# Where an early first layer puts its sums: three PSUM tiles in turn, or four banks of one tile

## The chip, the cores and the metric

The kernel runs on one core of a Trainium2 chip. The metric is the device time of one execution in microseconds (us). The engines have short names in the profile: PE is TensorE (matmuls), PEld its weight loads, DVE is VectorE, ACT is ScalarE, POOL is GpSimd, and SPq is the queue from which most DMA transfers are issued.

## What is computed

A chunked state-space block (Mamba-2 style) makes 3072 tokens of 256 numbers. A router sends each token to the one of eight experts whose embedding is closest by cosine; the expert is a two-layer network with a Relu between the layers.

```python
# reference, cut to what matters here
x = attn_out.transpose(0, 2, 1, 3).reshape(3072, 256)       # tokens from the state-space block
xn, en = normalized(x), normalized(expert_emb)
logits = xn @ en.T / tau
expert_idx = np.argmax(logits, axis=1)
gate_w = softmax(logits)[np.arange(N), expert_idx]
for e in range(8):
    mask = expert_idx == e
    h = np.maximum(x[mask] @ w1[e], 0.0)                     # first layer: 256 -> 1024
    out[mask] = gate_w[mask, None] * (h @ w2[e])             # second layer: 1024 -> 256
```

All numbers are 32-bit floats.

## The kernel before

The kernel has two parts. The first (`mamba`) makes the tokens chunk by chunk, finds the expert and the row of each token (`pick`, `locate`) and scatters the tokens to the rows of their experts in DRAM (`scatter`). The second (`moe`) reads each expert's rows back and runs the two layers.

To keep TensorE busy where the two parts meet, the tokens that are already there for the first two experts are loaded early, and the first expert's first layer is computed at the end of the first part, while the last chunk's tokens are still being located, counted and scattered:

```python
# end of mamba(k): eight hidden blocks, four before and four after the last chunk's bookkeeping
j = k.early[0]
for f in range(KF // 2):                 # KF = 8
    j.up(f, k.pg[:, f % 4, :])
j.measure()                              # squares on ScalarE, then a power on GpSimd
locate(k, NC - 1)                        # small matmuls into pz, VectorE reads them
count(k)                                 # one more small matmul into pz
scatter(k, NC - 1, 0, NB, None)          # four indirect DMAs issued by GpSimd
for f in range(KF // 2, KF):
    j.up(f, k.pg[:, f % 4, :])
j.prepare(k.early_has[:TR, 0, :])
```

One call of `up` is one hidden block of 128 units for 208 tokens: two accumulated products into PSUM, then a Relu which reads PSUM and writes `hT` in SBUF.

```python
def up(s, f, ps=None):
    ...
    t = (s.sum() if ps is None else ps)[:, 0:n]              # n = 208
    for j in range(KD):                                      # KD = 2
        nc.tensor.matmul(                                    # L745
            t, lhsT=s.w1[:, j, 128 * f : 128 * f + 128], rhs=s.xT[:, j, :], start=(j == 0), stop=(j == KD - 1)
        )
    if f % 2 == 0 or ps is not None:
        nc.scalar.activation(s.hT[:, f, :], t, ACT.Relu)     # L749
    else:
        nc.vector.tensor_scalar_max(s.hT[:, f, :], t, 0.0)   # L751
```

The first part's PSUM tiles fill all eight banks of 512 numbers:

```python
k.pg = ps.tile([128, 4, 512], F32, name="pg")        # four banks
k.py = ps.tile([128, 2 * KD, Q], F32, name="py")     # one bank, 4 x 128
k.pf = ps.tile([128, 512], F32, name="pf")           # one bank
k.pz = ps.tile([128, 2, 512], F32, name="pz")        # two banks
```

`pg` holds the products inside a chunk, `py` the outputs of a chunk, `pf` the states and, last, the early tokens turned by TensorE. `pz` is used by `locate` and `count`. Waits between engines are put in by the framework, from which instruction writes and reads which tile.

The second part starts by turning the second expert's early tokens (`turn_x`, L723), runs the first expert's second layer (L762), then the second expert's first layer with `sum` tiles from a pool of five (`sum`) and so on, expert by expert. Its pool takes over the PSUM banks of the first part. From the third expert on, the layers are computed with seven products in place of eight (L829), from weights that GpSimd mixes beforehand (L806).

```python
def moe(k):
    ...
    parts[1][0].turn_x()          # L723
    parts[1][0].turn_copies()
    leftover_blocks(k)
    parts[0][0].down(0, HT)       # L762
    for i in range(1, n):
        part(i)                   # up, turn the next tokens, down, out; loads for later parts
```

The late tokens of the first two experts, and the tokens of all others, are loaded (`xg`, L668) once the last scatter has landed.

Of the kernel before, what the change touches and what calls it, by code (L numbers as in the profile page):

```python
# [89 lines left out]
def load_decays(k):  # L90
    nc = k.nc
    k.a0 = k.mc.tile([128, 2, Q], F32, name="a0")
    nc.vector.memset(k.a0[64:128, 1, :], 1.0)
    a = k.a.rearrange("b h s -> (b h) s")
    for c in range(NC):
        (nc.sync if c % 2 else nc.scalar).dma_start(
            k.a0[32 * (c % 4) : 32 * (c % 4) + 32, c // 4, :], a[:, Q * c : Q * c + Q]
        )


def decays(k, kk):

    nc = k.nc
    tt = nc.vector.tensor_tensor
    a, f, r = k.a0[:, kk, :], k.f[:, kk, :], k.r[:, kk, :]
    nc.vector.tensor_scalar(out=a, in0=a, scalar1=1e-6, scalar2=1.0, op0=ALU.max, op1=ALU.min)
    at = k.mc.tile([128, 2], F32, name=f"at{kk}")
    nc.vector.tensor_copy(out=at[:], in_=a[:, 0:Q:HQ])
    nc.vector.memset(a[:, 0:Q:HQ], 0.0)
    nc.vector.tensor_tensor_scan(out=f, data0=a, data1=k.heads[:], initial=0.0, op0=ALU.mult, op1=ALU.add)  # L110
    w = k.mc.tile([128, 3], F32, name=f"w{kk}")
    tt(out=w[:, 0:1], in0=f[:, HQ - 1 : HQ], in1=at[:, 1:2], op=ALU.mult)
    nc.vector.reciprocal(out=r, in_=f)
    nc.vector.tensor_scalar_mul(r[:, 0:HQ], r[:, 0:HQ], w[:, 0:1])
    k.dec[kk] = at, w


def turn_decays(k, kk):

    nc = k.nc  # L120
    ps = k.pz[:, kk, 264:392]
    nc.tensor.transpose(ps, k.r[:, kk, :], k.ident[:])
    nc.scalar.copy(out=k.rT[:, kk, :], in_=ps)


def finish_decays(k, kk):


    nc = k.nc
    at, w = k.dec.pop(kk)  # L130
    f = k.f[:, kk, :]
    nc.vector.reciprocal(out=w[:, 1:2], in_=w[:, 0:1])
    nc.vector.tensor_scalar_mul(f[:, 0:HQ], f[:, 0:HQ], w[:, 1:2])
    nc.vector.tensor_tensor(out=w[:, 2:3], in0=w[:, 0:1], in1=at[:, 0:1], op=ALU.mult)
    nc.vector.tensor_scalar_mul(k.parts[:, 0, kk, :], k.block[:], f[:, Q - 1 : Q])
    nc.vector.tensor_scalar_mul(k.parts[:, 1, kk, :], k.block[:], w[:, 2:3])
# [24 lines left out]
def load_emb(k):  # L161
    nc = k.nc
    k.en = k.mc.tile([E, DM], F32, name="emb")
    nc.scalar.dma_start(k.en[:], k.emb)
    k.tau_t = k.mc.tile([E, 1], F32, name="tau")
    nc.scalar.dma_start(k.tau_t[:], k.tau.to_broadcast([E, 1]))
    k.en_r = k.mc.tile([E, 1], F32, name="emb_r")
    sq = k.mc.tile([E, DM], F32, name="emb_sq")
    nc.scalar.activation(sq[:], k.en[:], ACT.Square, accum_out=k.en_r[:])
# [22 lines left out]
def load(k, c):  # L192
    nc = k.nc
    t = Net()
    t.ct = k.inp.tile([128, NB, Q], F32, name="ct", tag="ct")
    t.b = k.inp.tile([128, NB, 128], F32, name="b", tag="b")
    t.x = k.inp.tile([128, NB, DM], F32, name="x", tag="x", bufs=4)
    for dst, src in ((t.b, k.B), (t.ct, k.CT), (t.x, k.x)):
        nc.sync.dma_start(dst[:].rearrange("p b m -> p (b m)"), src[c])
    k.ld[c] = t  # L200


def load_weights(k, e):
    k.w1t[e] = k.wp.tile([128, KD, F], F32, name="w1", tag="w1")
    k.nc.sync.dma_start(k.w1t[e][:], k.w1[e].rearrange("(k p) f -> p k f", p=128))
    k.w2t[e] = k.wp.tile([128, KF, DM], F32, name="w2", tag="w2")
    k.nc.sync.dma_start(k.w2t[e][:], k.w2[e].rearrange("(f p) m -> p f m", p=128))
# [7 lines left out]
def scale_b(k, p):  # L215

    nc = k.nc
    c, b, t = pair(k, p)
    s = k.un[p] = Net()
    s.bp = k.work.tile([128, 2, 128], F32, name="bp", tag="bp", bufs=3)  # L220
    g = 32 * (c % 4) + 8 * b
    r = k.rT[:, c // 4, g : g + 16].rearrange("p (b t q) -> p b t q", b=2, t=2)
    for v in range(2):
        nc.vector.tensor_tensor(
            out=s.bp[:].rearrange("p b (q t n) -> p b q t n", q=4, t=2)[:, :, :, v, :],
            in0=t.b[:, b : b + 2, :].rearrange("p b (q t n) -> p b q t n", q=4, t=2)[:, :, :, v, :],
            in1=r[:, :, v, :].unsqueeze(3).to_broadcast([128, 2, 4, N]), op=ALU.mult,
        )


def turn_b(k, p):

    for i in range(2):
        k.nc.tensor.transpose(k.pz[:, i, 264:392], k.un[p].bp[:, i, :], k.ident[:])
# [145 lines left out]
def mamba(k):  # L380
    nc = k.nc
    k.f = k.mc.tile([128, 2, Q], F32, name="f")
    k.r = k.mc.tile([128, 2, Q], F32, name="r")
    k.rT = k.mc.tile([128, 2, 128], F32, name="rT")
    k.parts = k.mc.tile([128, 2, 2, 4], F32, name="parts")
    k.tick = k.const.tile([1, 1], F32, name="tick")
    k.T, k.V, k.yT, k.dec, k.to = {}, {}, {}, {}, {}
    NP = NU // 2
    build_consts(k)
    load_decays(k)  # L390
    load(k, 0)
    load_emb(k)
    load(k, 1)
    decays(k, 0)
    turn_decays(k, 0)
    finish_decays(k, 0)
    scale_b(k, 0)

    for i in range(-2, NP + 2):
        new = i + 2 if i + 2 < NP else None  # L400
        out = i - 1 if 0 <= i - 1 < NP else None
        done = i - 2 if 0 <= i - 2 < NP else None
        c = (i + 2) // 2

        pick_now = (i - 3) // 2 if i % 2 and i >= 3 else None
        place_now = i // 2 - 2 if i % 2 == 0 and 4 <= i < NP else None
        if i % 2 == 0 and 2 <= i // 2 + 3 < NC:
            load(k, i // 2 + 3)
        if i == 1:
            fill_rows(k)  # L410
        if i in (2, 4, 7):
            load_weights(k, len(k.w1t))
        if place_now is not None:
            locate(k, place_now)
            if place_now == EC - 1:
                count_early(k)
        if new is not None:
            scale_c(k, new)
        if 0 <= i < NP:
            inner(k, i)  # L420
        if 4 <= i < NP:
            scatter(k, (i - 4) // 2, 2 * (i % 2), 2, done)
        if i == 2 * EC + 3:
            load_early(k)
        if i == 1:
            next_states(k, 0)
        elif i % 2 == 0 and 2 <= i and i // 2 < NC - 1:
            next_states(k, i // 2)
        if i == NP + 1:
            k.early[0].turn_x(k.pf)  # L430
        if done is not None:
            finish(k, done)
        if new is not None:
            turn_b(k, new)
        if done is not None:
            keep_tokens(k, done)
        if new is not None:
            keep_b(k, new)
        if out is not None:
            outputs_before(k, out)  # L440
        if new is not None and c < NC - 1:
            sums(k, new)
        if out is not None:
            outputs_within(k, out)
            keep_outputs(k, out)
        if pick_now is not None:
            pick(k, pick_now)
        if new is not None and i % 2 and c < NC - 1:
            states(k, c)
        if new is not None and new + 1 < NP:  # L450
            scale_b(k, new + 1)
        if i == -1:
            decays(k, 1)
            finish_decays(k, 1)
        if i == 0:
            turn_decays(k, 1)
            between(k)
        if i == 1:
            turn_emb(k)
            route_consts(k)  # L460
        if i == NP:
            locate(k, NC - 2)
            scatter(k, NC - 2, 0, NB, None)
    j = k.early[0]
    for f in range(KF // 2):
        j.up(f, k.pg[:, f % 4, :])
    j.measure()
    locate(k, NC - 1)
    count(k)
    scatter(k, NC - 1, 0, NB, None)  # L470
    for f in range(KF // 2, KF):
        j.up(f, k.pg[:, f % 4, :])
    j.prepare(k.early_has[:TR, 0, :])


# [59 lines left out]
def fill_rows(k):  # L535

    nc = k.nc
    none = k.work.tile([TR, NT * W], F32, name="none", tag="none", bufs=1)
    nc.gpsimd.memset(none[:], 1.0)
    for e in range(E):  # L540
        nc.sync.dma_start(k.rows[T * e : T * e + CAP, :].rearrange("(p t) w -> p (t w)", t=NT), none[:])
# [86 lines left out]
def load_early(k):  # L628
    k.early = [Job(k, HT, TR, k.w1t[e], k.w2t[e]) for e in range(EE)]
    for e, j in enumerate(k.early):  # L630
        if e == 0:
            j.pool, j.kept = k.ep, {}
        d = j.load(k.ep.tile([TR, HT, W], F32, name=f"xe{e}"), T * e)
        k.tc.add_to_no_dep_group("early", d.ins)
# [548 lines left out]
```

## Time and profile before

| what | value |
|---|---|
| time, median of three | 284.47 us (284.01 to 285.77) |
| span of the profiled execution | 283.5 us |
| mean granted TensorE clock | 0.98 |
| TensorE busy | 254.3 us, 90% of the span |
| early first layer, first product to the transposes after it | 85.67 to 96.80 us |
| TensorE busy in that stretch | 7.81 of 11.13 us |

A busy share is an average over stages that have different limits, so the stage that the change touches has to be looked at by itself: when each instruction starts, what it waited for, and whether the engine that is late there is also the one that the end of the kernel hangs on. Busy times of TensorE are modelled at their ends; starts are firmer.

### The profile page before, as it was taken

The numbers are of one execution on the slowest core, as the hardware profiler recorded it, in microseconds if no ns is written. First come the engines' busy times: TensorE is split into PE (matmuls) and PEld (weight loads), VectorE is DVE, ScalarE is ACT, GpSimd is POOL, SyncE is SP. The second block draws the span as 40 slices with busy tenths as digits, with TensorE's granted clock in tenths as the row PEclk, the third lists the DMA queues.
The fourth block names the chain that finished last, engine by engine and source line by source line (L and its number), as shares of the span: only waits on it lengthen the run. The fifth ranks groups of instructions, "written<-read, shape, count | busy, mean of one in ns | idle before, by whom it ended". The sixth has DMA issues, their size and how long they took to land. (4 is left out here: it accounts for less than half of the span.)

```text
span 283.5 us, 5813 instructions
## 1 busy us (share of the span) xinstructions
PE 254.3 (90%) x2084; PEld 232.0 (82%) x2084; DVE 182.5 (64%) x558; ACT 101.3 (36%) x306; POOL 156.2 (55%) x229
## 2 busy tenths in 40 slices
PE   0888999999977799999999999999999989999950
PEld 0566888887865699999999999999999979999940
DVE  7576798999733374333558668767767756866830
ACT  2322344345224222315154253343443434434310
POOL 8006418757425715856591498398398399323141
PEclk9999799999999999999999999999999999999995
DMA  4988398961132221066640371281190110001001
GB/s 157 367 307 300 84 375 288 384 233 59 43 106 79 79 66 30 15 175 231 210 154 21 82 281 40 65 313 43 44 333 28 38 59 26 27 9 53 0 28 31
DMA packets 18232, 37.30 MB, mean 132 GB/s; under 512 B 2042, under 2 KB 10439, under 8 KB 18202
## 3 DMA queue, kind: packets, MB, share of 16 engines
q1 hardware_dynamic: 15338, 30.36, 31.7%
q0 software_dynamic: 2688, 6.50, 6.9%
q8 instruction: 17, 0.28, 0.4%
q10 hardware_dynamic: 176, 0.06, 0.1%
q14 instruction: 13, 0.11, 0.1%
HBM read 26.80 MB, written 10.37 MB: 131 GB/s over the span
## 5 line engine op out<-in xcount | busy, mean ns | idle before, releaser
L785 POOL DMA_INDIRECT out_dram<-yo,to x32 | 34.5, 1078 | 19.5 <-DVE yo L781 13.8
L837 DVE TENSOR_TENSOR part<-sum,part 128x208 f32<-128x208 f32 x60 | 22.3, 371 | 25.7 <-ACT part L842 19.3
L595 POOL DMA_INDIRECT rows<-yt,row_of x24 | 23.9, 994 | 24.4 <-issue 11.8
L829 PE MATMUL sum<-dx,m 128*128 128x208 f32 x144 | 34.3, 350 | 0.0
L321 DVE TENSOR_TENSOR g<-pg,mask 128x1024 f32<-128x1024 f32 x24 | 28.2, 1217 | 5.6 <-PE pg L315 5.5
L806 POOL TENSOR_TENSOR m<-w 128x512 f32<-128x512 f32 x24 | 30.5, 1269 | 0.0
L837 DVE TENSOR_TENSOR h<-sum,part 128x208 f32<-128x208 f32 x72 | 25.0, 370 | 7.0 <-PE sum L829 4.4
L829 PEld LDWEIGHTS sum<-dx,m 128*128 128x128 f32 x144 | 24.9, 189 | 3.1 <-DVE part L837 2.5
L829 PE MATMUL sum<-dh,m 128*128 128x208 f32 x144 | 26.8, 342 | 0.5
L829 PEld LDWEIGHTS sum<-dh,m 128*128 128x128 f32 x144 | 25.0, 190 | 2.2 <-issue 1.9
L829 PE MATMUL sum<-xT,w 128*128 128x208 f32 x96 | 23.7, 340 | 1.0 <-DVEq L1067 1.0
L762 PE MATMUL sum<-hT,w 128*128 128x208 f32 x128 | 23.2, 340 | 0.0
L696 POOL TENSOR_TENSOR gr<-gr,half 104x4 f32<-104x4 f32 (+1 forms) x10 | 9.3, 935 | 23.7 <-ACT sq L692 23.7
L762 PEld LDWEIGHTS sum<-hT,w 128*128 128x128 f32 x128 | 22.3, 190 | 0.0
L842 ACT COPY part<-sum 128x208 f32<-128x208 f32 x36 | 11.9, 331 | 23.2 <-PE sum L829 23.2
L315 PE MATMUL pg<-cm,bt 32*128 32x256 f32 x192 | 19.9, 439 | 0.0
L983 POOL COPY tick<-gate 1x1 f32<-1x1 f32 x9 | 1.6, 178 | 32.2 <-DVE gate L714 32.2
L829 PE MATMUL sum<-h,w 128*128 128x208 f32 x96 | 18.8, 339 | 0.0
L260 ACT ACTIVATE cm<-cp,tmask 128x256 f32<-128x256 f32 x24 | 10.9, 500 | 20.9 <-DVE cp L255 20.9
L745 PE MATMUL sum<-xT,w 128*128 128x208 f32 x96 | 17.9, 339 | 0.0
L829 PEld LDWEIGHTS sum<-xT,w 128*128 128x128 f32 x96 | 16.7, 190 | 1.3 <-issue 1.3
L882 ACT ACTIVATE h<-h 128x208 f32<-128x208 f32 x24 | 9.0, 377 | 23.3 <-DVE h L837 23.3
(209 smaller groups left out, 554.1 us busy)
## 6 DMA issues: line engine op xcount, KB each, us to landing
w<-in_moe_w_dram SPq DMA_DIRECT2D x16, 1024.0 KB
rows<-none SPq DMA_DIRECT2D x8, 442.0 KB
x<-in_x_dram SPq DMA_DIRECT2D x6, 512.0 KB
xg<-rows SPq DMA_DIRECT2D x6, 442.0 KB
b<-in_B_dram SPq DMA_DIRECT2D x6, 256.0 KB
ct<-in_CT_dram SPq DMA_DIRECT2D x6, 256.0 KB
out_dram<-yo,to POOLq DMA_INDIRECT x32, 2.6
xe<-rows SPq DMA_DIRECT2D x2, 221.0 KB
```

What stands on the lines that cost most here:

```text
L260: nc.scalar.activation(s.cm[:, :, v, :], s.cp[:], ACT.Copy, scale=k.tmask[:, v : v + 1])
L315: nc.tensor.matmul(k.pg[:, q, 256 * i : 256 * i + 256], lhsT=s.bt[r, i, :], rhs=s.cm[r, i], start=True, stop=True, tile_position=(32 * q, 0),)
L321: nc.vector.tensor_tensor(out=g[:], in0=k.pg[:, :, 256 * i : 256 * i + 256].rearrange("p q (t i) -> p q t i", t=2), in1=k.mask[:].unsqueez ...
L595: d = nc.gpsimd.indirect_dma_start(out=k.rows[:, :], out_offset=bass.IndirectOffsetOnAxis(ap=k.to[g][:, u : u + 1], axis=0), in_=k.yt[:, N ...
L696: nc.gpsimd.tensor_tensor(out=s.r[:], in0=s.r[:], in1=k.half[0:tr, 0:nt], op=ALU.pow)
L745: nc.tensor.matmul(t, lhsT=s.w1[:, j, 128 * f : 128 * f + 128], rhs=s.xT[:, j, :], start=(j == 0), stop=(j == KD - 1))
L762: nc.tensor.matmul(t, lhsT=s.w2[:, f, 128 * j : 128 * j + 128], rhs=s.hT[:, f, c], start=(f == 0), stop=(f == KF - 1),)
L785: d = nc.gpsimd.indirect_dma_start(out=k.out[:, :], out_offset=bass.IndirectOffsetOnAxis(ap=s.to[:, i : i + 1], axis=0), in_=y[:], in_offs ...
L806: s.k.nc.gpsimd.tensor_tensor(out=out, in0=in0, in1=in1, op=op)
L829: s.k.nc.tensor.matmul(ps, lhsT=lhsT(i, g), rhs=rhs(j, g), start=(first and g == gs[0]), stop=(g == gs[-1]), skip_group_check=True,)
L837: s.k.nc.vector.tensor_tensor(out=out, in0=in0, in1=in1, op=ALU.add)
L842: s.k.nc.scalar.copy(out=out, in_=ps)
```

## The change

Three one-bank views take the place of the four banks of `pg`: the first bank of `pg`, all of `py` and all of `pf`. Block `f` goes to view `f % 3`. By then `py` and `pf` have done their work in the first part. The aim is that TensorE can write one block's sums while ScalarE still reads another's.

```diff
@@ -462,14 +462,15 @@
     j = k.early[0]
+    sums_at = (k.pg[:, 0, :], k.py[:].rearrange("p j q -> p (j q)"), k.pf[:])
     for f in range(KF // 2):
-        j.up(f, k.pg[:, f % 4, :])
+        j.up(f, sums_at[f % 3])
     j.measure()
     locate(k, NC - 1)
     count(k)
     scatter(k, NC - 1, 0, NB, None)
     for f in range(KF // 2, KF):
-        j.up(f, k.pg[:, f % 4, :])
+        j.up(f, sums_at[f % 3])
     j.prepare(k.early_has[:TR, 0, :])
```

## The prediction

> **What bounds the kernel now.** I read the page first, then busy time by stretches, then TensorE's waits and its timeline between 85 and 97 us, then GpSimd and the DMA queue beside it. The page's first part names the busiest engine:
>
> ```profile
> PE 254.3 (90%) x2084; PEld 232.0 (82%) x2084; DVE 182.5 (64%) x558; ACT 101.3 (36%) x306; POOL 156.2 (55%) x229
> ```
>
> An average does not tell where the other tenth is, so I cut the span where the change works: the early first layer is 85.67 to 96.80, and all that follows up to the last output copy is 97.22 to 269.07 (columns: stretch, length, busy time of PE, PEld, DVE, ACT, POOL with counts, granted clock, DMA share, GB/s).
>
> ```profile
> 85.67:96.80 11.13, 7.81 (x40) 5.37 (x39) 3.14 (x20) 4.31 (x14) 7.15 (x13) 1.00 0.20 75
> 96.80:108.93 12.13, 12.13 (x72) 12.05 (x73) 8.33 (x35) 3.02 (x11) 3.96 (x7) 1.00 0.25 79
> 97.22:269.07 171.85, 170.34 (x996) 163.88 (x995) 112.26 (x352) 64.92 (x223) 102.59 (x122) 1.00 0.31 98
> ```
>
> After the early layer TensorE is idle for 171.85 - 170.34 = 1.5 us out of 172: it is the bound there, and what reaches it sooner should end sooner. Inside the early layer it is idle for 3.3 us of 11.13. The waits of that stretch say for what (engine, line, waited for: us in total, times, longest us):
>
> ```profile
> PE pg L745 <- ACT hT L749: 2.6, 6, 0.4
> PE turned L723 <- ACT hT L749: 0.4, 1, 0.4
> PE pz L641 <- DVE oh L580: 0.3, 1, 0.3
> ```
>
> The timeline of TensorE shows the same as a rhythm (start us, us busy, what, idle before it and who ended it):
>
> ```profile
> 85.67 0.87 PE L745 MATMUL pg<-xT,w 128*128 128x208 f32 x4
> 86.97 0.97 PE L745 MATMUL pg<-xT,w 128*128 128x208 f32 x4 [0.43 <-ACT hT L749]
> 88.37 0.97 PE L745 MATMUL pg<-xT,w 128*128 128x208 f32 x4 [0.43 <-ACT hT L749]
> 89.78 0.97 PE L745 MATMUL pg<-xT,w 128*128 128x208 f32 x4 [0.43 <-ACT hT L749]
> ...
> 91.14 0.17 PE L641 MATMUL pz<-ob,ones_b 128*128 128x8 bf16 x1 [0.28 <-DVE oh L580]
> 91.18 0.97 PE L745 MATMUL pg<-xT,w 128*128 128x208 f32 x4
> ...
> 95.39 0.97 PE L745 MATMUL pg<-xT,w 128*128 128x208 f32 x4 [0.43 <-ACT hT L749]
> 96.80 0.58 PE L723 MATMUL turned<-ident,xe 104*128 104x104 f32 x4 [0.43 <-ACT hT L749]
> ```
>
> One hidden block (four matmul records) starts every 1.40 us: product, then the Relu that reads it out, then the next product. The next block is in another bank of `pg`, but it still waits for the Relu of the block before. For comparison, the same line L745 a little later, where each block gets its own `sum` tile:
>
> ```profile
> 104.71 4.38 PE L745 MATMUL sum<-xT,w 128*128 128x208 f32 x24
> 108.93 0.52 PE L723 MATMUL turned<-ident,xg 104*128 104x104 f32 x4
> ```
>
> 24 records from 104.71 to 108.93 are 4.22 / 24 = 0.176 us each, or 0.703 us per block, with no wait.
>
> **What the Trainium skill says.** "Perfetto Trace Analysis", section Matmuls, asks that independent groups rotate through PSUM banks so that reading one out overlaps the next group's matmuls. The kernel does rotate, and the 0.43 us waits show that this alone isn't enough here: the wait was put on the tile. "PSUM — Partial Sum Buffer", section on bank collisions, says that TensorE may write one bank while ScalarE reads another; the unbroken `sum` stage agrees. "Perfetto Trace Analysis", section Tensor Engine Instruction, warns that a matmul's end is an estimate, so I work from starts (0.703 us per block), not from durations (0.97 us). "TensorE: Matmul & The Clock Gate", Part 1, lets idle time of some 3.4 us lower the clock; the gaps here are 0.43 us and the clock reads 1.00 in all three stretches, so I count nothing for clock.
>
> **The change, part by part.** Compared instruction by instruction, nothing is added or removed: the same 16 products (32 records) and 8 Relus, in the same order, into other PSUM tiles. What changes is waits. Blocks 1 and 2 lose theirs altogether; blocks 3 to 7 keep one, but on the Relu of three blocks earlier. The transposes at L723 need the Relu of block 6 instead of block 7, and the second layer's eighth product waits for block 7's Relu, 7 x 2 x 0.176 = 2.5 us after the second layer starts, when that Relu (0.34 us) is over.
>
> Before, the starts are 85.67, 86.97, 88.37, 89.78, 91.18, 92.59, 93.99, 95.39 and 96.80 for the transposes: 11.13 us in all. After:
> - Blocks 0 to 3: three steps of 0.703 = 2.11 instead of 89.78 - 85.67 = 4.11. Gain 2.00.
> - Block 3 to block 4: the locate and count matmuls lie between, and the count (L641) waits for a VectorE product (L580) that reads locate's sums. That is a chain of its own: 89.78 to 91.14, with block 4 right behind. It stays 1.40. Gain 0. Locate's input (L561 on VectorE) ends at 87.84 and locate will come at about 88.5, so it does not hold.
> - Blocks 4 to 7 and on to the transposes: four steps of 0.703 = 2.81 instead of 96.80 - 91.18 = 5.62. Gain 2.81.
> - Sum: 2.00 + 0 + 2.81 = 4.81 us; the transposes start at about 92.0.
>
> Is ScalarE able to follow? A tile's own round is 1.40 us, and three tiles give one block per 0.47 us, under the 0.703 that TensorE takes. Two squares (L692, 1.04 us together) stand between the fourth and fifth Relu. The fourth Relu begins at about 88.7, so they end near 90.0; block 4 (start 89.18) is ready at about 90.05. Even a delay of 1 us would hold TensorE only at block 7, which needs block 4's tile.
>
> What goes along: the squares, GpSimd's power and the four last scatters hang on the end of block 3 and move 2.0 us, not 4.8. They matter because the loads of the late tokens wait for the scatters (GpSimd, then the DMA queue):
>
> ```profile
> 92.15 0.74 POOL L696 TENSOR_TENSOR gr<-gr,half 104x2 f32<-104x2 f32 x1 [2.89 <-ACT sq L692]
> 93.12 1.03 POOL L595 DMA_INDIRECT rows<-yt,row_of  x1 [0.17 <-DVE gr L707]
> 97.02 0.97 POOL L595 DMA_INDIRECT rows<-yt,row_of  x1 [0.21 <-issue]
> 99.60 23.20 SPq L668 DMA_DIRECT2D xg<-rows  x3
> ```
>
> Microsecond by microsecond, the DMA share falls to 0.05 at 103 to 104, so the load lands by about 103.2, and its first user is the transpose at 108.93: 5.7 us of room. After: landing at 101.2, user at 104.1, room 2.9 us. So the load stays hidden. Later weight loads, token loads and GpSimd's mixes are released by TensorE or by its followers, and move with it. I carry the 4.81 us to the end in full: 284.47 - 4.81 = 279.7 us, or 1.7% less.
>
> **The rivals.**
> 1. The late load becomes the new wait. If its landing kept its old time (103.2) there would still be 0.9 us of room, and it moves earlier. For it: the room halves. It would take about 3 us more than I reckon to show; then perhaps 281 to 282 us.
> 2. The gain is taken back later, by GpSimd's mixes (about 40% of GpSimd is free after 97 us) or by a weight load which does not move. Against it: in 172 us TensorE waits for no DMA, and the DMA queue itself waits for TensorE at L207 (4.2 and 3.2 us). It would make 281 to 284 us.
> 3. ScalarE, which has the squares between, passes less than I think, so only the first half gains: about 282.4 us. Against it: the three tiles of room.
> 4. More than I think: if locate and count were hidden too, the whole stretch would be 8 x 0.703 = 5.6 us, a gain of 5.5, 279.0 us. The L580 chain speaks against it.
>
> **Range and chances.** Faster by over 2% needs 284.47 x 0.02 = 5.69 us, more than even rival 4 gives; only the scatter between runs (284.01 to 285.77) could lend the rest. So faster by over 2% gets 0.08. Slower by over 2% has no mechanism: 0.01. Within 2%: 0.91. The range is 278.8 (rival 4 and a good run) to 281.8 (rival 1, or a high run).
>
> **What would show it.** Right: L745 into `pg`, `py`, `pf` starting every 0.70 us with no wait for ScalarE; the step from block 3 to 4 still near 1.4 us; the transposes at about 92.0; the last scatter some 2 us earlier and everything after block 7 some 4.8 us earlier, with TensorE idle for about 1.5 us after it as before. Wrong: TensorE waiting at L723 for the late tokens' load near 104 us (rival 1), new idle time at L829 (rival 2), or waits for Relu left in blocks 4 to 7 (rival 3).

## The result, and the profile after

The changed kernel takes 280.12 us, median of four (279.73 to 280.32), against 284.67 us before (284.01 to 285.77): a ratio of 0.9835, 95% interval 0.9801 to 0.9869. The profiled spans are 283.5 and 278.6 us. Lines of `kernel.py` from the change on are one higher than before (L745 is now L746, L749 is L750, and so on); an experiment that adds lines there moves them on further.

The timeline of TensorE in the changed kernel shows the early first layer (start us, us busy, what, idle before it and who ended it):

```profile
85.09 0.87 PE L746 MATMUL pg<-xT,w 128*128 128x208 f32 x4
85.80 0.87 PE L746 MATMUL py<-xT,w 128*128 128x208 f32 x4
86.50 0.87 PE L746 MATMUL pf<-xT,w 128*128 128x208 f32 x4
87.20 0.87 PE L746 MATMUL pg<-xT,w 128*128 128x208 f32 x4
...
88.46 0.17 PE L642 MATMUL pz<-ob,ones_b 128*128 128x8 bf16 x1 [0.28 <-DVE oh L581]
88.48 0.95 PE L746 MATMUL py<-xT,w 128*128 128x208 f32 x4
...
90.68 0.87 PE L746 MATMUL py<-xT,w 128*128 128x208 f32 x4
91.38 0.52 PE L724 MATMUL turned<-ident,xe 104*128 104x104 f32 x4
...
98.80 0.27 PE L779 MATMUL turned<-ident,yoT 128*104 128x128 f32 x1
99.44 0.54 PE L779 MATMUL turned<-ident,yoT 128*104 128x128 f32 x3 [0.37 <-DVE yoT L770]
```

Apart from the two steps around the count (1.28 and 0.79 us), a block starts every 0.70 us, and no block waits for ScalarE any more. The only wait left inside the stretch is the count's, for VectorE. The last line is new: the first expert's output transposes (L779) now wait for a VectorE copy, which they did not before. In the kernel before, the four ran together:

```profile
104.27 0.60 PE L778 MATMUL turned<-ident,yoT 128*104 128x128 f32 x4
```

The busy times by stretch, with cuts at the same events as for the kernel before (first block, early transposes, late tokens' transposes, and the last output copy, which is ScalarE's last copy into `yoT`, L922):

```profile
85.09:91.38 6.29, 6.01 (x40) 5.81 (x39) 3.15 (x20) 3.91 (x12) 4.82 (x8) 1.00 0.24 89
91.38:104.04 12.66, 12.29 (x74) 11.93 (x74) 8.52 (x35) 3.42 (x12) 6.25 (x12) 1.00 0.30 98
104.04:264.21 160.17, 158.65 (x927) 152.27 (x926) 104.29 (x318) 61.93 (x213) 98.86 (x116) 1.00 0.31 99
264.21:278.60 14.39, 4.03 (x24) 3.28 (x22) 2.44 (x9) 1.51 (x4) 4.59 (x9) 0.76 0.10 29
```

Set beside the kernel before, whose cuts are at 85.67, 96.80, 108.93 and 269.09 of 283.5 us, the whole difference of the two profiles is accounted for:

| stretch | before, us | after, us | difference |
|---|---|---|---|
| start to block 0 | 85.67 | 85.09 | -0.58 |
| block 0 to the early transposes | 11.13 | 6.29 | -4.84 |
| early to late transposes | 12.13 | 12.66 | +0.53 |
| late transposes to the last output copy | 160.16 | 160.17 | +0.01 |
| last output copy to the end | 14.41 | 14.39 | -0.02 |
| sum | 283.50 | 278.60 | -4.90 |

The first row is not the change's: up to block 0 both kernels run the same instructions, and this stretch varies by itself (last section). The change is worth 4.84 - 0.53, or 4.3 us.

### The profile page after: what moved, and what is told of

It is laid out like the page before. It is cut to its first block, busy times and chain, and to the rows that moved or that the text cites. A ratio compares the mean times of both kernels' runs of the same rounds, so it can differ in the third digit from the quotient of the medians.

```text
span 278.6 us, 5813 instructions
## 1 busy us (share of the span) xinstructions
PE 251.3 (90%) x2084; PEld 230.9 (83%) x2084; DVE 182.8 (66%) x558; ACT 101.2 (36%) x306; POOL 156.1 (56%) x229
## 5 line engine op out<-in xcount | busy, mean ns | idle before, releaser
L830 PE MATMUL sum<-dx,m 128*128 128x208 f32 x144 | 34.3, 350 | 0.0
L830 PEld LDWEIGHTS sum<-dx,m 128*128 128x128 f32 x144 | 24.9, 189 | 3.1 <-DVE part L838 2.5
L830 PE MATMUL sum<-dh,m 128*128 128x208 f32 x144 | 26.7, 342 | 0.5
L830 PEld LDWEIGHTS sum<-dh,m 128*128 128x128 f32 x144 | 25.0, 190 | 2.3 <-issue 1.9
L830 PE MATMUL sum<-xT,w 128*128 128x208 f32 x96 | 23.7, 340 | 1.0 <-DVEq L1068 1.0
L830 PE MATMUL sum<-h,w 128*128 128x208 f32 x96 | 18.8, 339 | 0.0
L746 PE MATMUL sum<-xT,w 128*128 128x208 f32 x96 | 17.9, 339 | 0.0
L830 PEld LDWEIGHTS sum<-xT,w 128*128 128x128 f32 x96 | 16.7, 190 | 1.3 <-issue 1.3
```

Of the source, the lines that this page charges most:

```text
L746: nc.tensor.matmul(t, lhsT=s.w1[:, j, 128 * f : 128 * f + 128], rhs=s.xT[:, j, :], start=(j == 0), stop=(j == KD - 1))
L830: s.k.nc.tensor.matmul(ps, lhsT=lhsT(i, g), rhs=rhs(j, g), start=(first and g == gs[0]), stop=(g == gs[-1]), skip_group_check=True,)
```

## The experiments

Each kernel differs from the changed one by the edit shown, except the second, which differs from the kernel before. Ratios are to the kernel before, run on the same chip. The stretches are read from the starts in each kernel's timeline of TensorE.

| kernel | ratio, 95% interval | block 0 to early transposes | early to late transposes | block 0 starts |
|---|---|---|---|---|
| two tiles | 0.9867, 0.9826 to 0.9908 | 6.40 | 12.96 | 85.65 |
| one bank | 0.9998, 0.9974 to 1.0022 | 11.13 | 12.13 | 87.09 |
| gate sooner | 0.9867, 0.9829 to 0.9905 | 6.29 | 12.07 | 86.26 |
| copy on ScalarE | 0.9879, 0.9815 to 0.9944 | 6.29 | 12.07 | 88.53 |
| first half only | 0.9936, 0.9916 to 0.9956 | 9.03 | 12.13 | 85.76 |
| second half only | 0.9924, 0.9905 to 0.9943 | 8.39 | 12.64 | 85.82 |
| gate sooner, count later | 0.9832, 0.9799 to 0.9864 | 5.95 | 12.16 | 85.06 |
| changed kernel again | 0.9900, 0.9878 to 0.9922 | 6.28 | 12.65 | 86.95 |

The first four rows ran on one chip, the last four on another. In these profiles block 0 starts anywhere within 3.5 us, and the totals move with it, so the stretches decide, not the ratios. Behind the two stretches little differs: from the late transposes to the end of the span every profile takes 174.4 to 174.6 us, except the copy on ScalarE (175.2). So from block 0 to the end the kernel before takes 197.8 us, and the changed kernel 193.5 us in both of its profiles.

**One bank: did four banks of one tile hide anything?**

```diff
-        j.up(f, k.pg[:, f % 4, :])
+        j.up(f, k.pg[:, 0, :])
```

> The kernel before with all eight blocks in pg's first bank. Theory (pg's four banks gave no overlap at all, since the wait is on the tile): the same time as the kernel before, ratio 0.997 to 1.003, a block every 1.40 us, stretch 11.1 us. Rival (the banks did hide a part, for instance a write beside a read): slower rhythm than 1.40 us and 1 to 3 us more in total.

Measured: no difference, 285.65 us against 285.58. Its timeline of TensorE is the old rhythm:

```profile
87.09 0.87 PE L745 MATMUL pg<-xT,w 128*128 128x208 f32 x4
88.39 0.97 PE L745 MATMUL pg<-xT,w 128*128 128x208 f32 x4 [0.43 <-ACT hT L749]
89.80 0.97 PE L745 MATMUL pg<-xT,w 128*128 128x208 f32 x4 [0.43 <-ACT hT L749]
...
98.22 0.57 PE L723 MATMUL turned<-ident,xe 104*128 104x104 f32 x4 [0.43 <-ACT hT L749]
```

From 87.09 to 98.22 is 11.13 us, as with four banks. So rotating through the banks of one tile bought nothing: here the waits follow the tile.

**Two tiles: is the third needed?**

```diff
-    sums_at = (k.pg[:, 0, :], k.py[:].rearrange("p j q -> p (j q)"), k.pf[:])
+    sums_at = (k.pg[:, 0, :], k.pf[:])
-        j.up(f, sums_at[f % 3])
+        j.up(f, sums_at[f % 2])
```

> Two PSUM tiles in turn (pg's first bank and pf) instead of three. Theory (the wait is on the tile; a tile's round of product, Relu and restart is 1.40 us): two tiles allow a block per 0.70 us, just what TensorE needs (0.703 us), so blocks start every 0.70 to 0.75 us and the stretch from block 0 to the transposes is 6.3 to 6.7 us (three tiles: 6.29 us); total within 0.4 us of the three tiles' time, about 0.984 to 0.986 of the kernel before. Rival (it takes more tiles because the Relu or its signal is slower than it looks): blocks 2, 3, 5, 6 and 7 wait for ScalarE by some tenths each, stretch 7.5 us or more, ratio 0.988 or more.

Measured: 6.40 us, 0.11 more than three tiles. The timeline of TensorE shows where:

```profile
89.83 0.87 PE L746 MATMUL pf<-xT,w 128*128 128x208 f32 x4
90.54 0.97 PE L746 MATMUL pg<-xT,w 128*128 128x208 f32 x4
91.35 0.87 PE L746 MATMUL pf<-xT,w 128*128 128x208 f32 x4
92.05 0.52 PE L724 MATMUL turned<-ident,xe 104*128 104x104 f32 x4
```

One step is 0.81 us (90.54 to 91.35): block 6 needs the Relu of block 4, and ScalarE's timeline has it from 90.15 to 90.49, just before block 6 starts.

```profile
90.15 0.34 ACT L750 ACTIVATE hT<-pg 128x208 f32<-128x208 f32 x1 [0.20 <-PE pg L746]
```

Block 6's first product record takes 0.443 us, as after a wait, instead of 0.339. The other steps are those of three tiles. A tile's round of 1.40 us over two tiles is just TensorE's 0.70, as the theory says, with no slack; the third tile gives some. The stretch after it is longer, 12.96 us: the transposes wait 0.67 us for VectorE's queue instead of 0.37. That is not shown to be the price of two tiles. The gate comes as soon after the early transposes as with three (0.68 us), but two small instructions of the queue, L714 and L1022, took 0.34 and 0.42 us in this profile instead of 0.17, for a reason not known.

**First half only, second half only: do the terms add up?**

```diff
# first half only: blocks 4 to 7 as before
-        j.up(f, sums_at[f % 3])
+        j.up(f, k.pg[:, f % 4, :])
# second half only: the same edit in the loop over blocks 0 to 3 instead
```

> Blocks 0 to 3 in three tiles, blocks 4 to 7 in pg's four banks as before. By the sum of the prediction: three steps of 0.703 us, one of about 1.3, four of 1.40, so 9.0 to 9.1 us from block 0 to the transposes (before 11.13, changed 6.29), a gain of 2.0 to 2.1 us. If the later wait at the first output transposes comes from TensorE running ahead of the last Relu (theory), it doesn't appear here, because the transposes wait for the last Relu again: 12.1 us from the early transposes to the late tokens' transposes, total about 0.993 of before. If it comes from the whole stretch being earlier (rival), some of it is seen here too, 12.3 to 12.7 us.

> Blocks 0 to 3 in pg's four banks as before, blocks 4 to 7 in three tiles. By the sum of the prediction: three steps of about 1.37 us, one of 1.3 to 1.4, four of 0.703, so 8.2 to 8.35 us from block 0 to the transposes, a gain of 2.8 us. Theory (TensorE ahead of the last Relu makes VectorE's queue late): the wait at the output transposes appears in full, 12.5 to 12.8 us from the early transposes to the late tokens' transposes, so net about 2.3 us or 0.992 of before. Rival (the whole stretch being earlier is the cause): less of it than in the changed kernel.

Measured: the first half gains 11.13 - 9.03 = 2.10 us, the second 11.13 - 8.39 = 2.74; the sum is 4.84, what the whole change gains. The medians do not add up so well (2.13 and 2.26 us below the kernel before, against 2.67 for the whole change on the same chip), and in the profile of the whole change block 0 starts 1.1 to 1.2 us later than in these two. The two also separate the cause of the new wait. It is absent with the first half only, where the early transposes wait for the last Relu as before, and there in full with the second half only. The two timelines of TensorE, first half only:

```profile
94.79 0.58 PE L724 MATMUL turned<-ident,xe 104*128 104x104 f32 x4 [0.43 <-ACT hT L750]
...
102.26 0.60 PE L779 MATMUL turned<-ident,yoT 128*104 128x128 f32 x4
```

and second half only:

```profile
94.21 0.52 PE L724 MATMUL turned<-ident,xe 104*128 104x104 f32 x4
...
102.25 0.54 PE L779 MATMUL turned<-ident,yoT 128*104 128x128 f32 x3 [0.36 <-DVE yoT L770]
```

So it isn't that the stretch as a whole is earlier, but that TensorE passes the last Relu.

**Gate sooner, and copy on ScalarE: is it VectorE's queue?** In the changed kernel VectorE's timeline shows what stands ahead of the copy that L779 waits for:

```profile
92.06 0.17 DVE L713 TENSOR_REDUCE gate<-gl 104x2 f32<-104x16 f32 x1 [1.24 <-ACT gl L711]
...
92.55 0.64 DVE L732 COPY xT<-turned 128x208 f32<-128x208 f32 x2
93.10 0.16 DVE L1018 TENSOR_SCALAR over<-n 128x8 f32<-128x8 f32 x1
...
98.96 0.14 DVE L1058 CAST table<-end 128x1 int32<-128x1 f32 x1
99.03 0.36 DVE L770 COPY yoT<-sum 128x208 f32<-128x208 f32 x1
```

VectorE is idle 1.24 us for the gate's Exp (L711), which ScalarE runs only after the last Relu. Then come the table of left-over blocks, 93.10 to 99.03 without a pause, and the copy. In the kernel before, the same table and copy were

```profile
97.87 0.16 DVE L1017 TENSOR_SCALAR over<-n 128x8 f32<-128x8 f32 x1
...
103.67 0.36 DVE L769 COPY yoT<-sum 128x208 f32<-128x208 f32 x1
```

The copy was over at 103.67 + 0.36 = 104.03, and the transposes started at 104.27. The first of the four reads only ScalarE's half of `yoT`; the second needs this copy, and comes about 0.11 us later (four in 104.71 - 104.27 = 0.44 us, L745 being next at 104.71). So the room was some 0.35 us. The two edits take the copy out of that queue, or the queue ahead of the last Relu:

```diff
# gate sooner
     for f in range(KF // 2, KF):
+        if f == KF - 1:
+            j.prepare(k.early_has[:TR, 0, :])
         j.up(f, sums_at[f % 3])
-    j.prepare(k.early_has[:TR, 0, :])
# copy on ScalarE, in down(); its new argument scalar is True only for the first expert's early tokens (call not shown)
-            if j % 2 == 0:
+            if j % 2 == 0 or scalar:
                 nc.scalar.copy(out=s.yT[:, j, c], in_=t)
```

> The changed kernel with the gate's work (prepare) put ahead of the last block, so that its Exp on ScalarE no longer stands behind the last Relu and VectorE reaches its table work sooner. Theory (the new wait of 0.37 us at the first output transposes is VectorE's queue, which hangs on the last Relu and the Exp behind it): VectorE starts the table work 0.5 to 0.6 us sooner, the wait goes, the stretch from the early transposes to the late tokens' transposes falls from 12.66 to about 12.15 us, total 0.5 us less than the changed kernel. Rival (the wait has another cause, such as the second layer's last product itself): stretch stays at 12.6 us.

> The changed kernel with the second copy of the first expert's second layer on ScalarE, which is idle then, instead of behind the table work on VectorE. Theory (VectorE's queue holds the copy up): the wait of 0.37 us at the output transposes goes, stretch from the early transposes to the late tokens' transposes 12.15 us instead of 12.66, total 0.5 us less than the changed kernel. Rival (the copy would be late on any engine): stretch stays at 12.6 us.

Measured: 12.07 us in both, and no wait at the output transposes. With the gate sooner, then with the copy on ScalarE:

```profile
99.96 0.60 PE L780 MATMUL turned<-ident,yoT 128*104 128x128 f32 x4
102.23 0.60 PE L779 MATMUL turned<-ident,yoT 128*104 128x128 f32 x4
```

With the gate sooner, VectorE's timeline reads:

```profile
92.52 0.17 DVE L714 TENSOR_REDUCE gate<-gl 104x2 f32<-104x16 f32 x1 [0.53 <-ACT gl L712]
...
93.56 0.33 DVE L1019 TENSOR_SCALAR over<-n 128x8 f32<-128x8 f32 x1
...
99.54 0.36 DVE L771 COPY yoT<-sum 128x208 f32<-128x208 f32 x1
```

Its early transposes start at 92.55, so the table begins 1.01 us after them instead of 93.10 - 91.38 = 1.72, and the copy 6.99 us after them instead of 7.65. In the kernel before it was 97.87 - 96.80 = 1.07 and 6.87. Both edits confirm the queue as the cause. The copy on ScalarE loses 0.68 us later (160.85 us from the late transposes to the last output copy, instead of 160.17); 0.5 us of it are waits for VectorE at L830, which the changed kernel doesn't have there, and whether the edit causes them was not followed.

**Gate sooner and count later: a version that is better still.**

```diff
     locate(k, NC - 1)
+    j.up(KF // 2, sums_at[KF // 2 % 3])
     count(k)
     scatter(k, NC - 1, 0, NB, None)
-    for f in range(KF // 2, KF):
+    for f in range(KF // 2 + 1, KF):
+        if f == KF - 1:
+            j.prepare(k.early_has[:TR, 0, :])
         j.up(f, sums_at[f % 3])
-    j.prepare(k.early_has[:TR, 0, :])
```

> The changed kernel with two more moves: the gate's work ahead of the last block, and the count's matmul after block 4 instead of before it. Theory: the step from block 3 to block 4 falls from 1.28 to 0.95 to 1.0 us since the count's wait for VectorE is hidden behind block 4, and the wait at the output transposes goes; stretch to the transposes about 6.0 us instead of 6.29, and 12.1 instead of 12.66 after it; total 0.8 us less than the changed kernel, about 0.981 of the kernel before. Rival: the count's wait only moves to another place (scatters or late loads), and no more than 0.5 us is gained.

> The changed kernel once more, beside the combined version on the same chip, for the comparison of the two: ratio to the kernel before about 0.984, 6.3 us to the transposes, 12.6 to 12.7 us after them.

Measured: 279.65 us (278.15 to 281.58), against 282.17 us (280.95 to 282.35) for the changed kernel beside it. The timeline of TensorE in the combined version:

```profile
87.17 0.87 PE L748 MATMUL pg<-xT,w 128*128 128x208 f32 x4
...
88.00 0.95 PE L748 MATMUL py<-xT,w 128*128 128x208 f32 x4
88.79 0.17 PE L644 MATMUL pz<-ob,ones_b 128*128 128x8 bf16 x1
88.81 0.95 PE L748 MATMUL pf<-xT,w 128*128 128x208 f32 x4
...
91.01 0.52 PE L726 MATMUL turned<-ident,xe 104*128 104x104 f32 x4
```

The count (L644) waits for nothing now. Block 3 to block 4 takes 0.83 us instead of 1.28, and block 4 to 5 takes 0.81. Both stretches together are 5.95 + 12.16 = 18.11 us, against 6.28 + 12.65 = 18.93: a gain of 0.82, as expected. The medians differ by 2.5 us, but the profiles put the rest ahead of the edits: block 0 starts there at 85.06 and 86.95 us, after identical instructions. The step from block 3 to block 4 fell further than the 0.95 to 1.0 us expected, and the changed kernel's ratio, 0.9900, missed the 0.984 expected of it.

## Why the prediction was right, step by step

- Blocks 0 to 3: 2.11 us predicted, 87.20 - 85.09 = 2.11 measured.
- Block 3 to block 4: 1.40 predicted, 1.28 measured. Some 0.1 us of the old step was the slower start after a wait: the first product record takes 0.443 us after idle time and 0.339 us in the flow.
- Blocks 4 to the transposes: 2.81 predicted, 91.38 - 88.48 = 2.90 measured; the step right after the count is 0.79 us.
- The sum: 6.32 predicted, 6.29 measured; the misses of the two terms above, 0.12 too long and 0.09 too short, nearly cancel. The term that makes up the gain was right in size and in mechanism.
- ScalarE keeps up: right; the fifth Relu begins at 89.47, right after the squares, and holds nobody up.
- The scatters come 2.0 us earlier, not 4.8: right. GpSimd's last scatter and the DMA queue's load behind it, in the changed kernel:

```profile
94.34 0.97 POOL L596 DMA_INDIRECT rows<-yt,row_of  x1 [0.22 <-issue]
97.83 20.08 SPq L669 DMA_DIRECT2D xg<-rows  x3
```

  The scatter is 97.02 - 94.34 = 2.68 us earlier, less the 0.58 by which block 0 was earlier: 2.10. The load begins only 99.60 - 97.83 = 1.77 us earlier, or 1.19.
- The late load stays hidden (against rival 1): right. TensorE does not wait for it at 104.04; the DMA share has fallen to 0.00 by 101 to 102 us.
- The gain is carried to the end in full, with 1.5 us of idle time on TensorE as before: this step failed, by 0.53 us. After block 7 TensorE waits for this:

```profile
PE sum L830 <- DVEq L1068: 1.0, 1, 1.0
PE turned L779 <- DVE yoT L770: 0.4, 1, 0.4
```

  The first was there before; the second is new. I checked how much room the late load had, but not how much VectorE's queue had, some 0.35 us. The queue hangs on the last Relu, which moved 96.40 - 91.58 = 4.82 us, while the early transposes moved 96.80 - 91.38 = 5.42: they no longer wait for that Relu. At the end of the queue the copy had moved 103.67 - 99.03 = 4.64 us and the output transposes 104.27 - 98.80 = 5.47. TensorE came 0.83 us nearer to its own follower, more than the room. Rival 2 (taken back later) had the right form, though not the place and only a ninth of the gain.

Predicted 279.7 us, measured 280.12. That the total came so near is partly luck, since it carries the time ahead of block 0, which the change does not touch. The second measurement of the same kernel is 282.17 us, 2.67 below its kernel before and above the top of the predicted range, 281.8. What both profiles bear out is the time from block 0 on: 197.8 - 193.5 = 4.3 us, of 4.81 predicted.

## What to carry to other kernels

Where a pool or a framework orders work by tiles, rotate through tiles, not through slices of one: four banks of one tile were worth no more than one bank (11.13 us in both), and two tiles almost as much as three, since a round of 1.40 us over two tiles meets the 0.70 us that TensorE needs. When an engine is freed from waiting for a follower, look at the follower's queue next: the room there shrinks by as much as the engine gains on it, and some 0.35 us of room was soon gone. A small result that waits for a read-back (the count) costs little if the next independent block stands before it: with it, the two steps around the count took 0.83 + 0.81 us here instead of 1.28 + 0.79.

## What was not expected of the hardware

The time to block 0, with the same instructions in all ten profiles, runs from 85.06 to 88.53 us, and with it go the two measurements of the changed kernel (0.9835 and 0.9900, medians 280.12 and 282.17 us; 85.09 and 86.95 us to block 0). In two of the three latest profiles (the changed kernel again, 86.95, and the copy on ScalarE, 88.53) many matmuls of 28 to 38 us are slower, though the granted clock is given as 1.00. From the groups of that window, the changed kernel again:

```profile
L315 PE MATMUL pg<-cm,bt 32*128 32x256 f32 x32 | 4.5, 526 | 0.0
```

and the combined version, where block 0 starts at 85.06:

```profile
L315 PE MATMUL pg<-cm,bt 32*128 32x256 f32 x32 | 2.7, 396 | 0.3 <-DVE g L321 0.3
```

The same 32 products take 526 ns on average instead of 396. In three other profiles (the kernel before, one bank, second half only) the recorded clock does fall, to between 0.50 and 0.56, at 30 to 32 us (columns as in the tables of stretches above). The kernel before, then the changed kernel:

```profile
30.00:32.00 2.00, 2.00 (x17) 1.67 (x20) 1.81 (x4) 0.68 (x2) 2.00 (x5) 0.50 0.09 34
30.00:32.00 2.00, 1.58 (x44) 1.34 (x46) 1.81 (x4) 0.68 (x2) 2.00 (x5) 1.00 0.04 13
```

Eight matmuls (L369) that start at 29.45 us in both hold TensorE 1.84 us in the kernel before and 1.03 in the changed one, by the start of what follows. By 38 us the kernel before is about 0.5 us behind, most of the 0.58 us in the first row of the table of differences. "TensorE: Matmul & The Clock Gate", Part 1, says that the clock is low until the array has been busy for a while and that the moment of release varies between runs of one kernel; that would fit, but it wasn't tested here, and for the changed kernel again and the copy on ScalarE the recorded clock doesn't show it. The clock is not all: the profile of one bank, with the same dip as the kernel before, starts block 0 1.42 us later, and right before it TensorE waits 1.72 us for the load of the early tokens instead of 0.87.
